# Linear attention and two expert layers on one core: a packed attention state, fewer groups of attention matmuls, other banks and other tiles for sums

## The chip, the cores and the metric

The kernel runs on one core of a Trainium2 chip. The metric is the device time of one execution in microseconds (us). TensorE (PE) has a clock with two levels, 1.2 and 2.4 GHz; the profile gives the granted share of the higher one.

## What is computed

A linear attention with a decaying state feeds a two-layer network with ELU, and that feeds four experts with ReLU, weighted by normalised probabilities. All is float32.

```python
# attention: batch 4, heads 8, 768 steps, head size 48
for t in range(S):
    state = alpha[:, :, t, :, None] * state + np.einsum('bhd,bhe->bhde', k[:, :, t], v[:, :, t])
    y[:, :, t] = np.einsum('bhd,bhde->bhe', q[:, :, t], state)
# first layer: 3072 tokens, 384 -> 2048 -> 384
h = x @ w_in
g = np.where(h > 0.0, h, np.exp(np.minimum(h, 0.0)) - 1.0)
x = g @ w_out
# second layer: 4 experts, 384 -> 1024 -> 384
p = domain_probs / (domain_probs.sum(-1, keepdims=True) + 1e-09)
for e in range(E):
    out += p[:, e:e + 1] * (np.maximum(x @ w1[e], 0.0) @ w2[e])
```

## The kernel before

**Units.** The 768 steps are cut into 6 chunks of 128. A unit is one chunk of one batch, 24 in all; each has 8 heads, two to a group of 128 partitions (head j of a pair on partitions 64j to 64j+47, the rest padding). For a unit, `prep0` to `prep2` make the running products of alpha by a scan (L181) and scale k and q with them (L198 to L208); `scores` multiplies k by q on TensorE (L218) into two banks, and VectorE masks them into `sm` (L224); `ktrans` transposes k (L235), and ScalarE copies it to `kn`; `yout_t` adds the state's part (L265) and the values' part (L272) in one bank, ScalarE copies it to `yt` (L277), it is stored to memory and read back in another layout as `xr` (L281); `state` multiplies `kn` by the values (L295) and updates the state of the batch on VectorE (L306, L308); the unit's `raw` tile is then free for the load of a later unit (L171); `xtrans` makes two halves of `xr`, a cast on ScalarE (L330) and a subtraction on VectorE (L331).

**The state** of a batch was a tile of 128 partitions x 4 pairs x 112 columns, with the two heads of a pair as diagonal blocks of 48 and zeros between, so that one matmul served both.

**First layer.** A block is one chunk of all batches, 512 tokens; it has 16 items. An item is nine matmuls of the first product (`first`, L370) into one bank of a ring of three (h0, h1, h2), the ELU (L381 to L383, and a split into `g` by ScalarE, L330, and VectorE, L331), and nine of the second product (`second`, L393) into t0 to t2, two items later. At a block's end ScalarE copies t0 to t2 to `x1raw` (L850). The units of the next chunk run between the items of a block: each has six steps, one in each half item. Weights of the first layer stand in the tiles W0 to W7 (two items each), the block's input in X0 or X1 by turns.

**Before and behind.** The four units of the first chunk run ahead of block 0, with five banks. The last block has no attention; during it GpSimd makes the 15 sums (`xs`, L497) of the first pair of chunks that the second layer multiplies, and each is split by a cast on ScalarE and a subtraction on GpSimd (`xc`). The second layer (L650, L700) uses 15 sums for 18 products; its weights are loaded by SP (`wa`, `wb`).

**Order.** TensorE's order is the program's in the first chunk and in the second layer; elsewhere a scheduler orders each engine's instructions from the program's order, its pools and its own estimates. Engines then work in order.

## Time and profile before

| | |
|---|---|
| median of 3 runs | 1308.62 us (1307.59 to 1314.47) |
| profiled execution | 1309.81 us, span 1308.1 us |
| TensorE busy | 1258.4 us, 96% |
| VectorE busy | 890.6 us, 68% |
| ScalarE busy | 582.7 us, 45% |
| GpSimd busy | 518.4 us, 40% |
| mean granted clock | 0.986 |

Times in rows are counted from the span's start. PE is the matmuls, PEld the weight loads, DVE is VectorE, ACT ScalarE, POOL GpSimd, SP the queue of loads. A matmul that follows another starts before that one has ended, so the cost of a group is read from starts: from its first start to the first start of what follows. A float32 matmul is recorded as two passes. The idle time before an instruction stands in brackets with what ended it.

### The profile page before, as it was taken

How to read it: one execution, taken by the hardware profiler on the slowest of the kernel's cores; microseconds unless marked ns; L12 is line 12 of the kernel's file. 1: busy time of each engine (PE TensorE's matmuls, PEld its weight loads, DVE VectorE, ACT ScalarE, POOL GpSimd, SP SyncE). 2: the span in 40 equal slices, each digit the busy share in tenths (PEclk: the TensorE clock that was granted, in tenths of full speed). 3: DMA queues.
4: the chain of work that ended last, by engine and by line, in shares of the span. 5: the costliest groups of instructions: out<-in, count | busy, mean ns of one | idle time of the engine just before them, and what ended most of it. 6: DMA issues, size and time to landing. Idle time of an engine off the chain costs nothing.

```text
span 1308.1 us, 17463 instructions
## 1 busy us (share of the span) xinstructions
PE 1258.4 (96%) x6297; PEld 1014.6 (78%) x6297; DVE 890.6 (68%) x1546; ACT 582.7 (45%) x1076; POOL 518.4 (40%) x405
## 2 busy tenths in 40 slices
PE   8989999999999998889999999899999999999997
PEld 5676788778778787668888888788888878888886
DVE  9999988687777742366757666566667575767664
ACT  5666666566556564433434241333333233333241
POOL 0000000000000015348878474887966465447472
PEclk9999999999999999999999999999999999999999
DMA  6545366556666541425747348765645574525232
GB/s 246 195 164 178 109 221 239 189 203 214 242 223 216 188 147 73 173 93 194 258 159 278 114 161 335 256 243 183 255 167 199 185 296 166 195 97 204 102 109 75
DMA packets 71533, 246.67 MB, mean 189 GB/s; under 512 B 6680, under 2 KB 38264, under 8 KB 62096
## 3 DMA queue, kind: packets, MB, share of 16 engines
q1 hardware_dynamic: 68016, 236.84, 50.5%
q10 hardware_dynamic: 3424, 8.65, 1.9%
q8 instruction: 51, 0.84, 0.3%
q14 instruction: 42, 0.34, 0.1%
HBM read 182.11 MB, written 63.36 MB: 188 GB/s over the span
## 4 chain that ended last, share of the span: by engine, by line
PE 65%; DMA 11%; DVE 11%; ACT 5%; POOL 5%; issue 2%; SPq 1%; ACTq 0%; DVEq 0%; POOLq 0%
PE h L650 22%; PE t L700 13%; PE a L700 9%; PE t L393 7%; PE h L370 7%; DMA wraw<-in_we_dram 5%; PE h L700 4%; DMA x0d<-yt 2%; DMA raw<-in_att_dram 2%; DVE u L670 1%; DMA xr<-x0d 1%; DVE wh L331 1%; DVE P L181 1%; POOL xs L497 1%; DVE h L383 1%
## 5 line engine op out<-in xcount | busy, mean ns | idle before, releaser
L670 DVE TENSOR_TENSOR u<-h,u 128x512 f32<-128x512 f32 x258 | 177.5, 688 | 90.4 <-PE h L650 89.4
L393 PE MATMUL t<-g,w_W 128*128 128x512 f32 x864 | 226.1, 404 | 13.1 <-ACT g L330 12.5
L370 PE MATMUL h<-x,w_W 128*128 128x512 f32 x864 | 224.0, 402 | 3.7 <-ACT w_W L330 3.7
L650 PE MATMUL h<-xc_Q,wa 128*128 128x512 f32 x780 | 219.9, 391 | 3.3 <-DVE g L331 1.4
L630 POOL TENSOR_TENSOR g_W<-c,g_W 128x512 fp32r<-128x512 f32 x128 | 164.8, 1303 | 123.6 <-ACT c L629 105.5
L393 PEld LDWEIGHTS t<-g,w_W 128*128 128x128 f32 x864 | 162.5, 192 | 53.0 <-ACT g L330 14.6
L628 ACT ACTIVATE g_W<-c 128x512 fp32r<-128x512 f32 x128 | 80.0, 626 | 274.5 <-DVE c L670 159.9
L370 PEld LDWEIGHTS h<-x,w_W 128*128 128x128 f32 x864 | 162.8, 192 | 42.5 <-ACT w_W L330 5.1
L331 POOL TENSOR_TENSOR xc_X<-xr,xc_X 128x512 fp32r<-128x512 f32 x2 | 2.6, 1300 | 478.9 <-DMA xr<-x1d 478.7
L650 PEld LDWEIGHTS h<-xc_Q,wa 128*128 128x128 f32 x780 | 145.4, 188 | 37.4 <-DVE u L670 3.8
L700 PE MATMUL t<-g_W,wb 128*128 128x512 f32 x576 | 157.6, 389 | 0.0
L700 PEld LDWEIGHTS t<-g_W,wb 128*128 128x128 f32 x576 | 108.0, 188 | 22.6 <-POOL g_W L630 0.2
L629 ACT ACTIVATE c<-c 128x512 f32<-128x512 f32 x192 | 121.0, 632 | 7.4
L670 DVE TENSOR_TENSOR c<-u,h 128x512 f32<-128x512 f32 x123 | 84.1, 686 | 50.4 <-PE h L650 38.4
L664 DVE COPY u<-h 128x512 f32<-128x512 f32 x99 | 68.1, 690 | 68.3 <-PE h L650 68.0
L700 PE MATMUL a<-g_W,wb 128*128 128x512 f32 x384 | 112.0, 391 | 0.0
L630 POOL TENSOR_TENSOR g_X<-c,g_X 128x512 fp32r<-128x512 f32 x64 | 82.5, 1303 | 62.6 <-ACT c L629 52.0
L628 ACT ACTIVATE g_X<-c 128x512 fp32r<-128x512 f32 x64 | 40.0, 626 | 142.0 <-DVE c L670 78.5
L383 DVE SCALAR_TENSOR_TENSOR h<-e,h 128x512 f32<-128x512 f32 x96 | 66.5, 692 | 49.7 <-ACT e L382 49.2
L331 DVE TENSOR_TENSOR g<-h,g 128x512 fp32r<-128x512 f32 x96 | 66.0, 687 | 37.7 <-ACT g L330 36.7
L650 PE MATMUL h<-xc_W,wa 128*128 128x512 f32 x297 | 85.0, 395 | 4.9 <-DVE u L670 2.9
L700 PEld LDWEIGHTS a<-g_W,wb 128*128 128x128 f32 x384 | 72.4, 188 | 15.4 <-POOL g_W L630 0.3
(150 smaller groups left out, 1965.1 us busy)
## 6 DMA issues: line engine op xcount, KB each, us to landing
wa<-wad SPq DMA_DIRECT2D x33, 1536.0 KB, 6.6
wb<-wbd SPq DMA_DIRECT2D x30, 1536.0 KB, 6.5
raw<-in_att_dram SPq DMA_DIRECT2D x22, 960.0 KB, 5.1
wad<-wh SPq DMA_DIRECT2D x44, 384.0 KB, 2.8
wbd<-wh SPq DMA_DIRECT2D x43, 384.0 KB, 3.4
xcd<-xh SPq DMA_DIRECT2D x30, 512.0 KB, 3.7
wraw<-in_wm_dram SPq DMA_DIRECT2D x16, 768.0 KB, 4.3
wraw<-in_we_dram SPq DMA_DIRECT2D x20, 576.0 KB, 5.3
```

The lines of the kernel that those rows point to most:

```text
L181: nc.vector.tensor_tensor_scan(P[:, a, :], raw[:, A0 + a * C:A0 + (a + 1) * C], self.plo.to_broadcast([128, C]), 1.0, ALU.mult, ALU.max,)
L331: (eng or nc.vector).tensor_tensor(out=lo, in0=src, in1=hi.bitcast(F32), op=ALU.subtract)
L370: nc.tensor.matmul(h[:, 0:n], w[:, wl, fi, k * 128:(k + 1) * 128], x[:, xl, k, n0:n0 + n], start=(k == 0 and i == 0), stop=(k == KD - 1 an ...
L383: nc.vector.scalar_tensor_tensor(out=h, in0=e, scalar=-1.0, in1=h, op0=ALU.add, op1=ALU.max)
L393: nc.tensor.matmul(self.xa[k][:, 0:n], w[:, wl, fi, DM + k * 128:DM + (k + 1) * 128], g[:, gl, 0:n], start=(f == 0 and i == 0), stop=(f == ...
L628: nc.scalar.activation(out=g[:, n, 0], in_=v, func=AF.Relu)
L629: nc.scalar.activation(out=v, in_=v, func=AF.Relu)
L630: nc.gpsimd.tensor_tensor(out=g[:, n, 1], in0=v, in1=g[:, n, 0].bitcast(F32), op=ALU.subtract)
L650: nc.tensor.matmul(b, w[:, wl], x[:, xl], start=(j == 0), stop=(j == 2))
L664: nc.vector.tensor_copy(out, b)
L670: (nc.vector if "b" in (a0, a1) or dst == "S5" else nc.gpsimd).tensor_tensor(out=out, in0=val(a0, b), in1=val(a1, b), op=ALU.add if op == ...
L700: nc.tensor.matmul(oa[m, d], wt[:, f, wl, d * 128:(d + 1) * 128], G[m][:, f, gl], start=first, stop=last)
```

## The change

The state holds 64 columns a pair, the two heads above each other on their partitions, with no zeros. The state's part of the output becomes two matmuls a pair (48 rows to 64 columns each, on separate halves of the array, into separate partitions of one bank). The state's own matmuls write 64 columns, padding included, so that its update is one addition and one product on all 128 partitions. The transposes take a bank of the first layer's ring and stand right behind the scores; `state` stands right behind `yout_t`; `prep1` one step earlier. The sums of the first pair use tile X0 in place of W1, begin in the program at the start of the last block and are spread over more of it, and W1 and X0 change places among the tiles of `xc` and `wa`. The ring of the first layer's banks shrinks to two one step later.

```diff
-            s = self.ap.tile([128, NP, SW], F32, tag=f"st{b}", name=f"st{b}")
+            s = self.ap.tile([128, NP, 64], F32, tag=f"st{b}", name=f"st{b}")
...
     def ktrans(self, u):
-        ps = self.abank()
+        ps = self.hbank()
...
         for a in range(NP):
-            nc.tensor.matmul(
-                ps[0:SW, a * C:(a + 1) * C], self.st[b][:, a, :], raw[:, Q0 + a * C:Q0 + (a + 1) * C],
-                start=(a == 0), stop=False, skip_group_check=True,
-            )
+            for j in range(2):
+                r = slice(64 * j, 64 * j + D)
+                nc.tensor.matmul(
+                    ps[64 * j:64 * j + 64, a * C:(a + 1) * C], self.st[b][r, a, :], raw[r, Q0 + a * C:Q0 + (a + 1) * C],
+                    start=(a == 0), stop=False, skip_group_check=True,
+                )
...
-        st = self.st[b]
+        st = self.st[b][:, :, 0:D]
...
-                ps[64 * j:64 * j + D, h // 2, 0:D],
-                kn[:, (h // 2) * C + 64 * j:(h // 2) * C + 64 * j + D],
+                ps[64 * j:64 * j + 64, h // 2, 0:D],
+                kn[:, (h // 2) * C + 64 * j:(h // 2) * C + 64 * j + 64],
...
+        src = ps[:, :, 0:D]
         if c:
             tmp = self.ap.tile([128, NP, D], F32, tag="tmp", name="tmp")
-        for j in range(2):
-            r, e = slice(64 * j, 64 * j + D), slice(64 * j, 64 * j + D)
-            src = ps[r, :, 0:D]
-            if c:
-                nc.vector.tensor_tensor(out=tmp[r], in0=src, in1=st[r, :, e], op=ALU.add)
-                src = tmp[r]
-            nc.vector.tensor_tensor(
-                out=st[r, :, e], in0=src, in1=pc[r].to_broadcast([D, NP, D]), op=ALU.mult
-            )
+            nc.vector.tensor_tensor(out=tmp, in0=src, in1=st, op=ALU.add)
+            src = tmp
+        nc.vector.tensor_tensor(out=st, in0=src, in1=pc.to_broadcast([128, NP, D]), op=ALU.mult)
...
-        s = [[(self.scores, (u,))]]
+        s = [[(self.scores, (u,))] + ([] if last else [(self.ktrans, (u,))])]
         s.append(N(self.prep0))
-        s.append([] if last else [(self.ktrans, (u,))])
-        s.append([(self.yout_t, (u,))] + N(self.prep1))
-        s.append([] if last else [(self.state, (u,))])
-        s[-1] += N(self.prep2)
+        s.append(N(self.prep1))
+        s.append([(self.yout_t, (u,))] + ([] if last else [(self.state, (u,))]))
+        s.append(N(self.prep2))
...
-        tmp = self.big.tile([128, 6, 512], F32, tag="W1", name="xs")
+        tmp = self.big.tile([128, 6, 512], F32, tag="X0", name="xs")
...
-        return ("Q0", "Q1", "Q2", "X0", "W0", "W5")[self.xn % 6]
+        return ("Q0", "Q1", "Q2", "W0", "W1", "W5")[self.xn % 6]
...
-        t = self.big.tile([128, 12, 2, 128], F32R, tag=("W2", "W1")[i % 2], name="wa")
+        t = self.big.tile([128, 12, 2, 128], F32R, tag=("W2", "X0")[i % 2], name="wa")
...
         def begin_x0():
-            for n, s in enumerate(self.prep_x0()):
-                at(b5 + 6 + n * 9 // 20, do, s)
-
-        at(b5 + 5, begin_x0)
+            x0 = self.prep_x0()
+            at(b5, do, x0[0])
+            for n, s in enumerate(x0[1:]):
+                at(b5 + 2 + n * 12 // 19, do, s)
+
+        at(b5 - 1, begin_x0)
...
-        self.hb = ("h0", "h1")
...
+            if i:
+                self.hb = ("h0", "h1")
```

In the changed kernel L366 and L389 are the two products of the first layer, L267, L274 and L297 the state's part, the values' part and the state, L377 and L378 the first two steps of the ELU, L327 and L328 the two halves of a split, L493 the sums.

TensorE in a unit of the third block, before, from the product behind the scores on (`a` are the attention's banks, `h` and `t` the first layer's):

```order
L370 MATMUL h_2638<-x_0_1516,w_W_874 128x512 x9
L235 MATMUL a_2655<-ident,raw 128x128 x4
L393 MATMUL t_2343<-g,w_W_748 128x512 x3
L393 MATMUL t_2344<-g,w_W_748 128x512 x3
L393 MATMUL t_2345<-g,w_W_748 128x512 x3
L265 MATMUL a_2671<-raw,st_152 112x128 x4
L272 MATMUL a_2671<-sm,raw 48x128 x8
L370 MATMUL h_2700<-x_0_1516,w_W_874 128x512 x9
L295 MATMUL a_2717<-raw,kn 48x48 x8
```

And now, from the last matmul of the scores on:

```order
L218 MATMUL a_2616<-raw 128x128
L235 MATMUL h_2629<-ident,raw 128x128 x4
L389 MATMUL t_2357<-g,w_W_652 128x512 x3
L389 MATMUL t_2358<-g,w_W_652 128x512 x3
L389 MATMUL t_2359<-g,w_W_652 128x512 x3
L366 MATMUL h_2661<-x_0_1522,w_W_874 128x512 x9
L389 MATMUL t_2357<-g,w_W_753 128x512 x3
L389 MATMUL t_2358<-g,w_W_753 128x512 x3
L389 MATMUL t_2359<-g,w_W_753 128x512 x3
L267 MATMUL a_2691<-raw,st_152 64x128 x8
L274 MATMUL a_2691<-sm,raw 48x128 x8
L297 MATMUL a_2714<-raw,kn 64x48 x8
```

The transposes moved up to the scores and into an `h` bank, and the state moved up to the output.

GpSimd at the start of the last block, now; ahead of these rows stand one sum (`xs<-xr`) and one split of an input (`xc_Q_4972<-xr`), so that the second of the pair at the end is the fifteenth of this chain:

```order
L493 TENSOR_TENSOR xs<-xr 128x512
L328 TENSOR_TENSOR xc_Q_5063<-xs,xc_Q_5063 128x512
L493 TENSOR_TENSOR xs<-xs,xr 128x512
L493 TENSOR_TENSOR xs<-xr 128x512
L328 TENSOR_TENSOR xc_Q_4898<-xs,xc_Q_4898 128x512
L493 TENSOR_TENSOR xs<-xs 128x512
L493 TENSOR_TENSOR xs<-xr,xs 128x512
L328 TENSOR_TENSOR xc_Q_4972<-xs,xc_Q_4972 128x512
L328 TENSOR_TENSOR xc_Q_4898<-xs,xc_Q_4898 128x512
L328 TENSOR_TENSOR xc_Q_4972<-xr,xc_Q_4972 128x512
L328 TENSOR_TENSOR xc_Q_4898<-xs,xc_Q_4898 128x512
L493 TENSOR_TENSOR xs<-xr 128x512 x2
```

Before, these sums stood behind the four splits that need no sum, and the chain had other tiles.

ScalarE at the end of a block's copies, before (`e<-h_4686` and `e<-h_4724` begin the ELU of two items of the last block):

```order
L381 ACTIVATE e<-h_4686 128x512
L382 ACTIVATE e<-e 128x512
L850 COPY x1raw<-t_4033 128x512
L850 COPY x1raw<-t_4034 128x512
L330 CAST g<-h_4686 128x512
L850 COPY x1raw<-t_4035 128x512
L851 DMA x1d_70<-x1raw 128x1536
L381 ACTIVATE e<-h_4724 128x512
```

And now (`e<-h_4688` and `e<-h_4749` belong to the first two items of the last block; the cast of `xc_Q_5063` just ahead of `e<-h_4749` reads the second of the pair of sums that ends the rows of GpSimd):

```order
L327 CAST xc_Q_4972<-xs 128x512
L377 ACTIVATE e<-h_4688 128x512
L327 CAST xc_Q_4898<-xs 128x512
L378 ACTIVATE e<-e 128x512
L327 CAST xc_Q_4898<-xs 128x512
L327 CAST xc_Q_5063<-xs 128x512
L327 CAST g<-h_4688 128x512
L327 CAST xc_Q_5063<-xs 128x512
L377 ACTIVATE e<-h_4749 128x512
L850 COPY x1raw<-t_4065 128x512
L378 ACTIVATE e<-e 128x512
L850 COPY x1raw<-t_4066 128x512
```

Casts of sums now stand ahead of the copies that free t0 to t2.

## Rows read from the trace of the kernel before

**Rows 1.** Busy by stage: stretch, length, PE, PEld, DVE, ACT, POOL, clock, DMA:

```profile
0.00:41.00 41.00, 34.90 (x281) 24.30 (x283) 36.35 (x76) 22.28 (x43) 1.09 (x8) 0.92 0.67 239
41.00:110.00 69.00, 61.81 (x365) 47.89 (x362) 63.87 (x105) 44.02 (x76) 0.00 (x0) 0.93 0.53 179
481.00:557.00 76.00, 67.59 (x282) 54.54 (x281) 22.14 (x32) 36.76 (x63) 33.13 (x27) 0.96 0.32 115
```

**Rows 2.** Waits of PE, 175 to 475: sum, times, longest (us):

```profile
PE a L235 <- DVE sm L224: 8.3, 5, 2.8
```

**Rows 3.** Timeline of PE, one unit: start, length, instructions:

```profile
178.38 1.16 PE L218 MATMUL a<-raw 48*128 48x128 f32 x16
179.47 2.34 PE L393 MATMUL t<-g,w_W 128*128 128x512 f32 x9
...
186.22 1.03 PE L265 MATMUL a<-raw,st 128*112 128x128 f32 x8
...
188.19 2.34 PE L370 MATMUL h<-x,w_W 128*128 128x512 f32 x9
190.46 0.56 PE L295 MATMUL a<-raw,kn 128*48 128x48 f32 x16
190.96 2.34 PE L393 MATMUL t<-g,w_W 128*128 128x512 f32 x9
```

**Rows 4.** Timeline of PE, two other units:

```profile
28.59 1.16 PE L218 MATMUL t<-raw 48*128 48x128 f32 x16 [0.51 <-PE a L248]
29.68 0.66 PE L235 MATMUL t<-ident,raw 128*128 128x128 f32 x4
...
119.67 1.08 PE L272 MATMUL a<-sm,raw 128*48 128x128 f32 x16
120.58 0.53 PE L295 MATMUL a<-raw,kn 128*48 128x48 f32 x16
121.04 1.19 PE L393 MATMUL t<-g,w_W 128*128 128x512 f32 x4
```

**Rows 5.** VectorE by line: op, count, busy us, mean ns:

```profile
L308 DVE TENSOR_TENSOR st<-tmp,P 48x192 f32<-48x192 f32 x32 | 11.3, 352 | 0.9
```

**Rows 6.** Timeline of ACT, DVE and PE, 287 to 292:

```profile
287.45 0.51 ACT L330 CAST x<-xr 128x384 fp32r<-128x384 f32 x1 [3.82 <-DMA xr<-x0d]
...
288.81 0.67 DVE L331 TENSOR_TENSOR g<-h,g 128x512 fp32r<-128x512 f32 x1
...
290.73 0.66 PE L235 MATMUL a<-ident,raw 128*128 128x128 f32 x4 [1.86 <-DVE sm L224]
```

**Rows 7.** Timeline of the SP queue, 277 to 286:

```profile
278.15 0.42 SPq L171 DMA_DIRECT2D raw<-in_att_dram  x1
284.94 0.37 SPq L281 DMA_DIRECT2D xr<-x0d  x1
```

**Rows 8.** Timeline of PE in the last block, and its waits, 474 to 575:

```profile
489.27 2.20 PE L370 MATMUL h<-x,w_W 128*128 128x512 f32 x9
...
513.75 2.20 PE L370 MATMUL h<-x,w_W 128*128 128x512 f32 x9
...
534.49 2.20 PE L370 MATMUL h<-x,w_W 128*128 128x512 f32 x9
...
PE t L393 <- ACT g L330: 8.2, 2, 4.6
```

**Rows 9.** Timeline of POOL in the last block:

```profile
505.83 2.55 POOL L497 TENSOR_TENSOR xs<-xr 128x512 f32<-128x512 f32 x2 [19.56 <-PE t L393]
508.34 1.29 POOL L497 TENSOR_TENSOR xs<-xs,xr 128x512 f32<-128x512 f32 x1
```

**Rows 10.** Timeline of ACT in the last block:

```profile
481.58 0.62 ACT L330 CAST xc_Q<-xr 128x512 fp32r<-128x512 f32 x1 [0.68 <-DMA xr<-x1d]
```

**Rows 11.** Load issues of the page: count, KB, us to landing:

```profile
wa<-wad SPq DMA_DIRECT2D x33, 1536.0 KB, 6.6
```

**Rows 12.** Timeline of PE at the start of layer 2:

```profile
560.52 1.65 PE L650 MATMUL h<-xc_Q,wa 128*128 128x512 f32 x6 [1.39 <-DVE g L331]
```

More of the change, by code (lines that the diff above doesn't have):

```diff
@@ L502, in prep_x0 @@
         x, s = {}, {}
-        tiles = [self.xc_tile() for _ in range(5)]
-        at = {p: (tiles[i // 3], i % 3) for i, p in enumerate(ORDER)}
+        tiles = []
         def loads(k):
@@ L528, in one @@
         def one(p):
-            t, i = at[p]
+            i = ORDER.index(p)
+            if i % 3 == 0:
+                tiles.append(self.xc_tile())
+            t, i = tiles[i // 3], i % 3
             y = s[p] if p in s else v[p] if p in v else x[XSUM[p][0]]
```

## The prediction

> **What bounds the kernel now.** I read the busy time by stage first [rows 1]: TensorE works 61.8 of 69 us in the stretch 41 to 110 us and 67.6 of 76 us in 481 to 557 us, so time comes from taking its waits away; but VectorE works 36.4 of the first 41 us and 63.9 of the 69 us after it, so there VectorE sets the pace. The rest of the span, from 557 us on, is the second layer, whose instructions stand in the same order on every engine after the change but for the first group and a few tile names; I leave it alone. Next the waits of TensorE between 175 and 475 us [rows 2]: one line stands out, the key transposes that wait for VectorE's masking (`sm`), 8.3 us in 5 waits. The timeline of one unit [rows 3, 4] gives the price of each group of attention matmuls. The last two places are the block 481 to 557, with 8.2 us of waits for ScalarE [rows 8], and the first step of layer 2, which waits 1.39 us for a bank [rows 12].
>
> **The span and the median.** The profiled execution took 1309.81 us with a span of 1308.1; the median of the runs is 1308.62. I sum against the profiled one and take the difference off the median.
>
> **The array's own time.** Nine matmuls of the first layer take 2.04 us (a first and a second product follow each other every 4.08 us: 489.27 to 513.75 is six such pairs, [rows 8]). Moving the transposes behind the scores costs and saves nothing: the scores take 1.09 us up to the next matmul of the layer (178.38 to 179.47, [rows 3]), and also 1.09 us up to transposes that follow them directly (28.59 to 29.68, [rows 4]), so the change of mode is only paid elsewhere. Output and state took 1.97 (186.22 to 188.19) and 0.50 us (190.46 to 190.96), together 2.47. Now the state part of the output is made of eight matmuls on two 48-row halves instead of four on the whole array, in the form of the scores; if pairs run side by side as there, it takes 1.09 us. The values part takes 0.91 (119.67 to 120.58) and the state right behind it 0.46 (120.58 to 121.04), as the one unit shows in which they already stood together [rows 4]. That is 2.46: nothing gained inside. What goes is one exit and one entry: 188.19 to 190.46 is 2.27 for nine matmuls, 0.23 over. The split state part brings an entry of its own, about half of that. So 16 units gain 0.1 to 0.15 each, the four last ones (no state) lose about 0.2 each, and in the first block, where the scheduler puts pieces of first-layer products between the pieces of two units, I count a loss of up to 1. I take -1, bounds -3 and +1.
>
> The pairing is the unknown: no row shows two row halves that write different partitions of one bank. The scores pair two row halves into two banks; the values part pairs two column halves in one bank. Both run paired, so I take paired. Unpaired, the eight pairs (1.09 less the change of mode, 0.2, is 0.89) take 0.89 more, over 20 units 17.8 us.
>
> The rows show pairs of row halves only with a bank each. The Trainium skill (TensorEngine Tiling (Array Packing), Restrictions and Gotchas, "Gotcha 1: PSUM Pressure") says more: row tiles must write to different banks and cannot be in one bank at the same time. No run shows it either way; by that rule the unpaired price holds, which is the first rival.
>
> **VectorE.** A state update on two halves was two products of 0.352 us [rows 5] and two additions of the same shape, which I count alike; on all 128 partitions it is one of each. In the first chunk a unit loses one product (4 x 0.352 = 1.4 us before 41 us); each of the 16 later units loses 0.704. VectorE is the bound up to 110 us and somewhat beyond, where four of these lie: 2.8. Later the saving is covered by VectorE's own slack. 4.2 us is the most; as the order there changes on all engines, I take -3, bounds -5 and +3.
>
> **The transposes' bank.** Before, they took one of two banks that the scores had just filled, and so waited for the mask. Now they take a bank of the first layer, which is free: the 8.3 us go. What is late next is the same bank pool. With the transposes in the ring of three, the second product group after the scores finds its bank used by the group just ahead of the scores, and must wait until VectorE's subtraction of that group has read it. In the unit at 290 us that subtraction starts at 288.81 and takes 0.67, ending at 289.48 [rows 6]; TensorE would be there 1.86 us before 290.73 plus the 0.4 of the transposes that it has done earlier, at 289.3: 0.2 us of wait in place of 1.86. The subtraction is late since ScalarE, and VectorE with it, stood behind the cast of `xr`, 3.82 us [rows 6]. That cast waits for a store and a read through memory: the raw load goes out at 278.15, the read of `xr` only at 284.94 [rows 7], since the store queues with the load's 128 x 1920 floats. Merging output and state lets the raw load go out 2 to 3 us sooner, as soon as the state has read its tile; the store then finds the load further on. On the other side the new ScalarE order puts that cast ahead of the exponential, which delays the group by 1 us if `xr` is no earlier, and where the store used to go ahead of the load it now goes behind. So 0 to 1.3 us a unit stay in some six units. I take 1.3 in all and -7; bounds -8.3 (nothing stays) and -2 (each pays most).
>
> SP's queue matters here: `xr` now stands behind one store of converted weights, which waits for VectorE; that store is ready sooner than the attention store lands, so I give it nothing.
>
> **The sums of the first pair.** Before, GpSimd could not start them until 505.83 [rows 9], when weights tile W1 was free, and ScalarE stood in order behind them: TensorE lost 34.49 less two periods, 534.49 - 513.75 - 8.16 = 12.6 us, of which 8.2 are waits [rows 8] and the rest the granted clock, 0.96 of the stage [rows 1]. Now they use X0, free after the block's predecessor, so GpSimd can start when the first inputs are in: ScalarE's first cast that waits for `xr` starts at 481.58 [rows 10]. GpSimd needs 1.255 us an instruction (505.83 to 508.34 is two, [rows 9]). The order decides the rest. ScalarE's cast of `xc_Q_5063<-xs` that stands just ahead of `e<-h_4749` needs the fifteenth instruction of GpSimd: 481.6 + 15 x 1.255 = 500.4. Behind it on ScalarE come that activation and then the copy `x1raw` of bank t0, each 0.6: t0 is free at about 502.2, t2 at 503.8. The second product of the block's first group starts in t0, and TensorE reaches it at 491.31 (489.27 plus 2.04). So it waits 10.9 us, in one piece, and ends at 504.5 instead of 493.35: 11.1 lost. The clock, which read 0.96 over this stage with two waits of four us, will have fallen: 1 to 2.5 us more. That makes 12.1 to 13.6 against 12.6: I take 0, bounds -1.5 and +3. No other wait follows: the casts into W0 and W1 stand where their sums have long been made. On SP the weight load into X0 now stands ahead of the other `wa` and waits for GpSimd's last read of the sums, its thirtieth instruction, at about 520 us; it, the other and two `wb` behind it take under 7 us each [rows 11] and are needed from 557 on, so they are covered, by some 9 us.
>
> **The first step of layer 2** keeps three banks instead of two, so the 1.39 us wait [rows 12] goes. The step after it reuses the bank of the step before once, about 1 us for VectorE. I take -1; bounds -1.4 and 0.
>
> **Sum:** -1 - 3 - 7 + 0 - 1 = -12. 1309.81 becomes 1297.8, the median 1308.6 becomes **1296.6**; I say 1296.5. Adding the bounds in the same direction is too wide; half of their widths gives 1288 to 1304 for this case alone.
>
> **Rivals.** (1) Slower: the two row halves do not run together in one bank. 17.8 us on top of the sum: 1314. It decides from some two thirds of the 17.8 on, when the gain of 12 is eaten. For it: no row shows this form. Against it: the halves' outputs lie on different partitions, as in the values part, which pairs. (2) The bank wait only moves: the groups behind the transposes wait as long as the transposes did, and VectorE's saving is lost in the new order; -1 and -1 remain: 1306.5. For it: both engines stand in order behind the cast of `xr`, and the new order puts that cast earlier. Against it: VectorE works less and the raw load is earlier. (3) The sums do what they were moved for: ScalarE's order does not bind and the 12.6 us go as well: 1284. For it: GpSimd starts 24 us sooner. Against it: the fifteenth instruction and the copy behind it, above.
>
> **How the numbers follow.** The forecast 0.66, rival (1) 0.08, rival (2) 0.19, rival (3) 0.07. Faster by over 0.5% (below 1302.1, about what a measurement of this kernel can tell from no change): most of the forecast, 0.62, and rival (3), 0.07: 0.69. Slower by over 0.5% (above 1315.2): part of rival (1), 0.04. The rest, 0.27, lies between. The range 1284 to 1307 leaves out rival (1), a third of rival (2) and half of rival (3), under 2 in 10.
>
> **What would show it.** Right: no wait of the transposes for `sm`; waits of the second group after the scores for VectorE's subtraction, together under 3 us; a raw load within 0.5 us of the output's end and the `xr` read near seven us after it; a unit's state part in pairs some 0.11 us apart, one after the other; VectorE with half the state updates at the same 0.35 us; one wait of about 11 us at the first second product of the last block, behind `x1raw`, with the clock at half speed after it; layer 2 as long as before. Wrong: single starts 0.11 us apart in the state part (rival 1), long waits of first products for banks (rival 2), a last block without a wait (rival 3), or a first 120 us that is longer than before, which would say that VectorE's work was not the bound there.

## The result, and the profile after

The changed kernel took 1297.93 us (median of 4 runs, 1294.08 to 1298.62); the kernel before beside it 1309.99. The ratio is 0.9898, with a 95% interval of 0.9863 to 0.9933. A second series gave 0.9928 (0.9904 to 0.9952, 12 runs). The forecast was 1296.5, with a range of 1284 to 1307. The sum came out; its terms did not all come out, so the hit is in part luck, and that is what the rest is about.

Cut at the starts of three groups of matmuls (first product of the first layer, of its second block, of its last block) and at the first group of layer 2, the span reads as follows. Both kernels were profiled twice.

| stretch | before | changed | difference of the means |
|---|---|---|---|
| first chunk | 39.99, 40.07 | 42.56, 43.05 | +2.8 |
| block 0 | 99.71, 98.80 | 92.98, 92.63 | -6.5 |
| blocks 1 to 4 | 341.41, 340.40 | 336.35, 336.25 | -4.6 |
| last block, to layer 2 | 79.41, 80.16 | 78.95, 77.55 | -1.5 |
| layer 2 and end | 747.58, 747.67 | 745.78, 747.05 | -1.2 |

Busy time by these stretches in the kernel before, first execution (columns as in [rows 1]: length, PE, PEld, DVE, ACT, POOL, granted clock, DMA share, GB/s):

```profile
0.00:39.99 39.99, 33.89 (x271) 23.53 (x271) 35.52 (x75) 21.60 (x43) 1.09 (x8) 0.91 0.66 235
39.99:139.70 99.71, 90.13 (x527) 69.17 (x527) 92.47 (x153) 61.45 (x105) 0.00 (x0) 0.93 0.48 163
139.70:481.11 341.41, 332.37 (x2018) 267.25 (x2017) 260.19 (x570) 210.00 (x446) 0.66 (x1) 1.00 0.60 208
```

The same in the changed kernel, first execution:

```profile
0.00:42.56 42.56, 38.05 (x271) 26.56 (x271) 33.45 (x71) 21.68 (x43) 1.09 (x8) 0.84 0.60 212
42.56:135.54 92.98, 86.42 (x559) 66.39 (x559) 88.72 (x145) 60.65 (x106) 0.00 (x0) 1.00 0.52 179
135.54:471.89 336.35, 329.87 (x2145) 266.35 (x2144) 251.77 (x545) 207.53 (x445) 0.00 (x0) 1.00 0.61 211
471.89:550.84 78.95, 68.19 (x289) 55.91 (x288) 22.20 (x33) 38.16 (x66) 33.61 (x27) 0.91 0.32 116
```

Length less PE's busy time is what TensorE waited. In blocks 1 to 4 that went from 9.0 to 6.5 us, in block 0 from 9.6 to 6.6. In block 0 the clock matters as much: at 0.93 of 99.71 us up to 7.0 us were lost to it, at 1.00 none. The first chunk goes the other way, 0.91 to 0.84: up to 6.8 us lost in place of 3.6. From the start to block 1 the clock cost up to 10.6 and 6.6 us in the two executions of the kernel before, and 6.8 and 6.9 in the changed one.

The gain of 4.6 us in blocks 1 to 4 is less firm than the table looks. Three kernels of the experiments below have the order of instructions of one of the two in blocks 0 to 4. First the kernel before with the sums alone changed, then the changed kernel with the splits on VectorE, and with sums and splits there, each in blocks 1 to 4:

```profile
134.40:473.92 339.52, 332.03 (x2018) 267.40 (x2016) 261.77 (x573) 209.57 (x446) 0.00 (x0) 0.99 0.60 210
```

```profile
135.20:474.27 339.07, 331.32 (x2146) 267.58 (x2144) 251.96 (x545) 207.53 (x445) 0.00 (x0) 0.99 0.61 210
134.16:475.63 341.47, 332.83 (x2145) 268.66 (x2144) 252.32 (x545) 207.79 (x445) 0.00 (x0) 0.99 0.61 208
```

The old order thus waited 9.0, 6.8 and 7.5 us, the new one 6.5, 6.0, 7.8 and 8.6, and over these seven executions the stretch differs by 2.2 us and not by 4.6. In block 0 the same seven give 95.96 to 99.71 us against 92.63 to 93.10.

The waits of TensorE in blocks 1 to 4, changed kernel (sum, times, longest), which answer [rows 2]:

```profile
PE h L366 <- DVE g L328: 5.6, 4, 2.0
PE t L389 <- DVE g L328: 0.8, 2, 0.5
```

The 8.3 us of the transposes are gone, and 6.4 us stand in their place, at the next product groups. One unit, on PE, answers [rows 3]:

```profile
277.56 1.16 PE L218 MATMUL a<-raw 48*128 48x128 f32 x16
...
278.65 0.66 PE L235 MATMUL h<-ident,raw 128*128 128x128 f32 x4
...
287.69 1.09 PE L267 MATMUL a<-raw,st 48*64 48x128 f32 x16
...
288.71 1.08 PE L274 MATMUL a<-sm,raw 128*48 128x128 f32 x16
...
289.62 0.62 PE L297 MATMUL a<-raw,kn 128*64 128x48 f32 x16
...
290.17 2.14 PE L389 MATMUL t<-g,w_W 128*128 128x512 f32 x8
```

Scores to transposes 1.09, state part 1.02 (287.69 to 288.71), values part 0.91, state 0.55. The state part's eight pairs run side by side.

### The profile page after: what moved, and what is told of

Read it like the earlier page. It is cut to its first block, busy times and chain, and to the rows that moved or that the text cites. A ratio compares the mean times of both kernels' runs of the same rounds, so it can differ in the third digit from the quotient of the medians.

```text
span 1296.6 us, 17731 instructions
## 1 busy us (share of the span) xinstructions
PE 1252.3 (97%) x6457; PEld 1013.4 (78%) x6457; DVE 876.4 (68%) x1510; ACT 579.5 (45%) x1076; POOL 518.5 (40%) x405
## 4 chain that ended last, share of the span: by engine, by line
PE 68%; DMA 10%; DVE 10%; POOL 4%; ACT 4%; issue 3%; SPq 1%; ACTq 0%; DVEq 0%; POOLq 0%
PE h L648 22%; PE t L698 13%; PE a L698 9%; PE h L366 7%; PE t L389 7%; PE h L698 4%; DMA x0d<-yt 3%; DMA raw<-in_att_dram 2%; DMA wraw<-in_we_dram 2%; DMA xr<-x0d 1%; DVE wh L328 1%; DVE u L668 1%; DVE h L379 1%; DVE g L328 1%; PE a L267 1%
## 5 line engine op out<-in xcount | busy, mean ns | idle before, releaser
L389 PE MATMUL t<-g,w_W 128*128 128x512 f32 x864 | 220.3, 396 | 16.0 <-ACT x1raw L850 10.8
L366 PE MATMUL h<-x,w_W 128*128 128x512 f32 x864 | 218.5, 395 | 7.8 <-DVE g L328 5.6
L389 PEld LDWEIGHTS t<-g,w_W 128*128 128x128 f32 x864 | 161.4, 189 | 53.9 <-ACT x1raw L850 11.2
L493 POOL TENSOR_TENSOR xs<-xr 128x512 f32<-128x512 f32 x8 | 10.1, 1274 | 471.0 <-DMA xr<-x1d 471.0
L366 PEld LDWEIGHTS h<-x,w_W 128*128 128x128 f32 x864 | 160.3, 189 | 45.6 <-DVE g L328 7.3
L648 PE MATMUL h<-xc_W,wa 128*128 128x512 f32 x390 | 110.2, 391 | 4.6 <-DVE u L668 2.6
L628 POOL TENSOR_TENSOR g_X<-c,g_X 128x512 fp32r<-128x512 f32 x64 | 82.7, 1304 | 62.6 <-ACT c L627 51.7
L648 PEld LDWEIGHTS h<-xc_W,wa 128*128 128x128 f32 x390 | 72.7, 188 | 22.2 <-DVE u L668 4.0
L328 DVE TENSOR_TENSOR g<-h,g 128x512 fp32r<-128x512 f32 x96 | 65.9, 687 | 30.5 <-ACT g L327 30.2
```

Of the source, the lines that this page charges most:

```text
L328: (eng or nc.vector).tensor_tensor(out=lo, in0=src, in1=hi.bitcast(F32), op=ALU.subtract)
L366: nc.tensor.matmul(h[:, 0:n], w[:, wl, fi, k * 128:(k + 1) * 128], x[:, xl, k, n0:n0 + n], start=(k == 0 and i == 0), stop=(k == KD - 1 an ...
L389: nc.tensor.matmul(self.xa[k][:, 0:n], w[:, wl, fi, DM + k * 128:DM + (k + 1) * 128], g[:, gl, 0:n], start=(f == 0 and i == 0), stop=(f == ...
L628: nc.gpsimd.tensor_tensor(out=g[:, n, 1], in0=v, in1=g[:, n, 0].bitcast(F32), op=ALU.subtract)
L648: nc.tensor.matmul(b, w[:, wl], x[:, xl], start=(j == 0), stop=(j == 2))
```

## The experiments

Each kernel differs from one of the two by the edit shown. Medians and ratios are against runs of the kernel before on the same chip in the same series; 91 such runs have a median of 1309.2 us and a mean granted clock of 0.9864, and the changed kernel's 16 runs 1298.8 us and 0.9893.

| kernel | runs | median | ratio (95%) |
|---|---|---|---|
| before, bank of the transposes alone | 10 | 1306.34 | 0.9993 (0.997 to 1.0015) |
| before, packed state alone | 7 | 1318.14 | 1.0079 (1.0049 to 1.0108) |
| before, sums alone | 10 | 1309.09 | 0.9998 (0.9976 to 1.002) |
| changed, old steps of a unit | 10 | 1305.89 | 0.996 (0.9937 to 0.9983) |
| changed, state update in halves | 10 | 1311.44 | 1.0009 (0.9983 to 1.0035) |
| changed, two tiles for the running products | 10 | 1303.80 | 0.996 (0.9936 to 0.9984) |
| the same, raw loads held back | 4 | 1289.39 | 0.9854 (0.9822 to 0.9885) |
| changed, splits on VectorE | 6 | 1295.25 | 0.9897 (0.9864 to 0.993) |
| changed, sums and splits on VectorE | 4 | 1288.05 | 0.9815 (0.9771 to 0.9859) |
| both groups of edits | 4 | 1285.20 | 0.981 (0.9771 to 0.985) |

### The bank of the transposes alone

```diff
     def ktrans(self, u):
-        ps = self.abank()
+        ps = self.hbank()
```

> The kernel before with one edit: the key transposes take a bank of the first layer's ring, at their old step. Theory (the bank frees the transposes and part of the wait moves to the ring): no wait of the transposes for the masking is left in 175 to 475 us (8.3 us before), and waits of first products for VectorE's subtraction of 3 to 7 us appear in their place; the time falls by 1 to 5 us, to 1304 to 1308. Rival (the wait simply goes): no such new waits, about 8 us less, near 1300. Rival (it moves whole): as much wait as before, 1308 to 1310.

Its waits of TensorE in blocks 1 to 4:

```profile
PE h L370 <- DVE g L331: 5.2, 4, 2.5
PE t L393 <- DVE g L331: 0.9, 1, 0.9
PE t L393 <- ACT g L330: 0.3, 1, 0.3
```

6.4 us of new waits for 8.3 of old ones, as the first theory had it; the time is not told from the kernel before. Over three executions of the old code the waits for `sm` were 8.3, 6.8 and 7.5 us, so by the waits the bank by itself is worth 0.4 to 1.9 us, 1.1 on the mean.

### The packed state alone, and the changed kernel with the old steps

```diff
-            s = self.ap.tile([128, NP, SW], F32, tag=f"st{b}", name=f"st{b}")
+            s = self.ap.tile([128, NP, 64], F32, tag=f"st{b}", name=f"st{b}")
...
-        for j in range(2):
...
+        nc.vector.tensor_tensor(out=st, in0=src, in1=pc.to_broadcast([128, NP, D]), op=ALU.mult)
```

> The kernel before with the packed state alone: two matmuls a pair for the state's part of the output, 64 columns a pair, one addition and one product for the update; old steps, old banks, old sums. Theory (VectorE sets the pace up to 110 us): VectorE's busy time falls by 36 x 0.35 = 12.6 us, and the stretch from the first product of the first layer to the start of its second block, 99.7 us before, shortens by 2 to 4 us beyond what the granted clock explains; the rest stays: 1304 to 1307. Rival (the stretch is set by the granted clock, which fell five times in it before and not once after): no shortening where the clock is as low as before, 1307 to 1310. State part in pairs, with no extra 0.9 us a unit.

Blocks 1 to 4 of this kernel (busy time), the wait of its transposes, and the longest of them on VectorE and TensorE:

```profile
130.81:482.05 351.24, 337.42 (x2146) 266.76 (x2144) 252.23 (x549) 209.78 (x446) 0.66 (x1) 0.99 0.59 203
```

```profile
PE a L235 <- DVE sm L224: 13.0, 8, 4.0
```

```profile
266.78 1.37 DVE L181 TENSOR_TENSOR_SCAN P<-raw,plo 128x128 f32<-128x128 f32 x4 [5.11 <-DMA raw<-in_att_dram]
...
270.01 1.12 PE L235 MATMUL a<-ident,raw 128*128 128x128 f32 x4 [3.96 <-DVE sm L224]
```

A miss for both theories: slower than before by 0.8%. Two things are in the rows. TensorE's busy time is 5.0 us over the 332.37 of before, of which the clock can be 3.5 (0.01 of 351): so 1.5 to 5.0 us are the price of the split state part on its own. And the transposes wait for the mask longer, 13.0 us, although VectorE works less (252.2 against 260.2 us): in the engines' new order the mask stands behind other work that waits for a transfer, at 266.78 behind a scan that waits 5.11 us for its raw tile. In block 0 this kernel takes 93.79 us at a clock of 0.98, so a part of the gain there is with it.

```diff
-        s = [[(self.scores, (u,))] + ([] if last else [(self.ktrans, (u,))])]
+        s = [[(self.scores, (u,))]]
         s.append(N(self.prep0))
-        s.append(N(self.prep1))
-        s.append([(self.yout_t, (u,))] + ([] if last else [(self.state, (u,))]))
-        s.append(N(self.prep2))
+        s.append([] if last else [(self.ktrans, (u,))])
+        s.append([(self.yout_t, (u,))] + N(self.prep1))
+        s.append([] if last else [(self.state, (u,))])
+        s[-1] += N(self.prep2)
```

> The changed kernel with the old six steps of a unit: the transposes (in the first layer's bank) and the state each on its own between groups of first-layer matmuls. Theory (each group of attention matmuls costs TensorE a way in and out, so the merging pays and the split state part by itself costs): TensorE's own time in the four blocks after the first, waits taken off, is 4 to 7 us longer, near the 73.7 us over the first layer's matmuls that the packed state alone has, against 67.5 of the changed kernel; the bank waits stay at 5 to 8 us; time 1302 to 1306. Rival (the merging is worth little, and the gain is VectorE's and the bank's): under 2 us longer, 1297 to 1300.

Its blocks 1 to 4:

```profile
133.71:480.10 346.39, 337.49 (x2145) 267.78 (x2144) 252.16 (x546) 210.43 (x446) 0.04 (x1) 0.99 0.59 206
```

7.6 us more of TensorE's busy time than the 329.87 of the changed kernel; the clock (0.01 of 346) can be 3.5 of that, so 4 to 7.6 us are the matmuls' own. The waits are 8.9 us against 6.5. The two groups a unit thus carry the packed state: without them it costs TensorE more than it brings.

### VectorE's work given back

```diff
-        nc.vector.tensor_tensor(out=st, in0=src, in1=pc.to_broadcast([128, NP, D]), op=ALU.mult)
+        for j in range(2):
+            r = slice(64 * j, 64 * j + 64)
...
+            nc.vector.tensor_tensor(out=st[r], in0=src, in1=pc[r].to_broadcast([64, NP, D]), op=ALU.mult)
```

> The changed kernel with the state's update in two halves again (64 partitions each, two additions and two products), so that VectorE alone has its old work back: 36 more instructions of 0.35 us, 12.6 us. Theory of the prediction (VectorE sets the pace up to 110 us): the time from the start to the second block of the first layer, 135.5 us, grows by 2 to 4 us at the same granted clock. Rival (nothing there rests on VectorE's sum of work; the gain in this stretch was the clock): it stays within 1 us at the same clock; time 1296 to 1299.

Busy time in block 0 and in blocks 1 to 4, and then the timeline at a wait in block 2, on VectorE, ScalarE and TensorE:

```profile
41.36:137.11 95.75, 88.92 (x560) 67.15 (x559) 90.76 (x149) 61.16 (x105) 0.00 (x0) 0.98 0.50 174
137.11:482.55 345.44, 332.88 (x2146) 268.69 (x2144) 262.25 (x573) 208.57 (x445) 0.00 (x0) 0.99 0.60 206
```

```profile
246.77 1.37 DVE L181 TENSOR_TENSOR_SCAN P<-raw,plo 128x128 f32<-128x128 f32 x4 [5.87 <-DMA raw<-in_att_dram]
...
248.17 0.63 ACT L187 ACTIVATE lnP<-P 128x512 f32<-128x512 f32 x1 [6.16 <-DVE P L181]
...
249.24 1.22 PE L370 MATMUL h<-x,w_W 128*128 128x512 f32 x2 [4.30 <-DVE g L332]
```

The start of block 1 moves by 1.6 us (137.11 against 135.54) at nearly the same clock (0.88 and 0.98 in the two stretches up to there, against 0.84 and 1.00), under the 2 to 4 of the theory and over the rival's 1. The surprise is later: in blocks 1 to 4 TensorE waits 12.6 us instead of 6.0 to 8.6, and the whole advantage over the kernel before is gone. Not all of it is VectorE's arithmetic. The edit moves VectorE's order too, and the row at 246.77 shows the form of the loss: a scan stands in order ahead of the subtraction that TensorE needs, waits 5.87 us for its raw tile to land, and ScalarE stands behind the scan. How the loss divides between work and order was not separated. In block 0 the waits are 6.8 us (95.75 less 88.92), hardly more than the 6.2 to 6.6 of the changed order.

### Where the remaining bank wait comes from

In the changed kernel the waits look like this, on SP, ACT, DVE and PE:

```profile
271.68 0.48 SPq L171 DMA_DIRECT2D raw<-in_att_dram  x1
272.53 0.79 ACTq L281 DMA_DIRECT2D x0d<-yt  x2
...
278.84 1.37 DVE L181 TENSOR_TENSOR_SCAN P<-raw,plo 128x128 f32<-128x128 f32 x4 [1.78 <-DMA raw<-in_att_dram]
...
279.15 0.37 SPq L283 DMA_DIRECT2D xr<-x0d  x1
...
281.74 0.52 ACT L327 CAST x<-xr 128x384 fp32r<-128x384 f32 x1 [0.86 <-DMA xr<-x0d]
282.16 0.63 ACT L378 ACTIVATE e<-e 128x512 f32<-128x512 f32 x1
...
284.66 0.69 DVE L328 TENSOR_TENSOR g<-h,g 128x512 fp32r<-128x512 f32 x1
...
285.40 2.36 PE L366 MATMUL h<-x,w_W 128*128 128x512 f32 x9 [1.98 <-DVE g L328]
```

Two suspects stand ahead of `g`: the cast of `xr`, with the second step of the ELU right behind it (282.16), and a scan that had waited 1.78 us for a raw load. Both stand so ahead of three of the four long waits (200, 285 and 372 us); ahead of the fourth (329) VectorE and ScalarE stood waiting for a load of weights. The first edit takes the scan out of the way, the second also the load:

```diff
-        P = self.ap.tile([128, NP, C], F32, tag="P", name="P", bufs=3)
+        n = u[0] * B + u[1]
+        m = n % 3 if n < B else (n + 1) % 2 if n > B else 1
+        P = self.ap.tile([128, NP, C], F32, tag=f"P{m}", name="P")
```

> The changed kernel with one edit: the running products of alpha of the later units have two tiles by turns instead of three, so that a unit's scan can't stand ahead of the previous unit's state. Seen in the trace of the changed kernel: each of the long bank waits left (1.76 us at 198, 2.14 at 283, 1.32 at 328, 1.14 at 371 us) follows a scan that waited 0.2 to 1.8 us for its raw tile to land, with ScalarE's logarithm behind it and the first layer's exponential behind that. Theory A (this scan, hoisted to the landing of its load, makes ScalarE late): the waits of 7.4 us in 175 to 475 us fall under 2 us and the four blocks after the first shorten by 4 to 6 us; time 1291 to 1294. Theory B (the cast of xr, which waits for a store and a read, makes it late by itself, as the prediction had it): the waits stay at 5 to 8 us, 1296 to 1299.

```diff
+            if c * B + b > B + 2:
+                self.nc.gpsimd.tensor_copy(t[0:1, 0:1], self.xl[0:1, 0, 0:1])
             self.nc.sync.dma_start(out=t, in_=self.att[c, b])
...
-        y = self.y.pop(u)
+        y = self.xl = self.y.pop(u)
```

> The kernel of the run with two tiles for the running products, and with the raw loads of the later units held back: GpSimd copies one element of xr into the raw tile first, so that the load starts only when the read of xr has landed. Theory (the store before xr queues with the raw load, and ScalarE's cast of xr, which waits for both transfers, makes the first layer's ELU late): from the issue of the store to the issue of the xr read it takes 2 to 3.5 us instead of 4 to 6.3, the bank waits in the four blocks after the first fall from 7.5 to 1 to 4 us, and these blocks take 332 to 336 us. Rival (other transfers, of the weights of layer 2 above all, hold the store just as long, or the scan now waits for the later landing): the waits stay at 6 us or more.

The wait in blocks 1 to 4, first with the scan gated alone, then with the loads held back as well, and of the latter a piece of the timeline (the queues of ScalarE and SP, and GpSimd):

```profile
PE h L368 <- DVE g L330: 6.9, 5, 2.5
```

```profile
PE h L370 <- DVE g L332: 4.0, 3, 2.7
```

```profile
270.27 1.50 ACTq L285 DMA_DIRECT2D x0d<-yt  x2
...
274.52 0.37 SPq L287 DMA_DIRECT2D xr<-x0d  x1
...
277.24 0.17 POOL L172 COPY raw<-xr 1x1 f32<-1x1 f32 x1 [18.98 <-DMA xr<-x0d]
277.44 0.33 SPq L173 DMA_DIRECT2D raw<-in_att_dram  x1
```

The scan is not the cause: with it gated the wait is as long, since ScalarE then stands longer in front of the cast (its waits for `xr` between 135 and 472 us go from 6.9 to 19.2 us in all). The transfers are: with the load behind the read of `xr`, the store at 270.27 is through by 274.52 (4.3 us, against 6.6 from 272.53 to 279.15 above). From the second half's store to the read, the twelve units of blocks 1 to 3 average 3.7 us, against 4.6 with the scan gated alone and 5.0 in the changed kernel; the waits fall to 4.0 us (4.4 in the kernel with both groups of edits), blocks 1 to 4 to 334.52, and the time to 1289.39, of which 5.4 us come from the last block (73.58 us, with 6.5 us of wait for `x1raw` in that order). The second edit moves the order of VectorE and ScalarE too, and that share was not taken apart. As far as that goes, the prediction's chain (store, load, read, cast) holds. What it got wrong is that the change would shorten it: before, the average was 4.6. The first edit by itself measured slower than the changed kernel (1303.80); its blocks 1 to 4 took 339.17 us and its last block 83.31, where the wait for `x1raw` was 12.8 us. Why that wait differs between these two was not followed up.

### The sums of the first pair

The sums' part of the change alone, on the kernel before (tile X0, the early start, the tiles changed round):

```diff
-        tmp = self.big.tile([128, 6, 512], F32, tag="W1", name="xs")
+        tmp = self.big.tile([128, 6, 512], F32, tag="X0", name="xs")
...
-        at(b5 + 5, begin_x0)
+            x0 = self.prep_x0()
+            at(b5, do, x0[0])
+            for n, s in enumerate(x0[1:]):
+                at(b5 + 2 + n * 12 // 19, do, s)
+
+        at(b5 - 1, begin_x0)
```

> The kernel before with the sums of the first pair alone changed (tile X0, earlier in the program, spread; the tiles of the inputs and of a weight changed round). Theory (ScalarE stands in order behind GpSimd's 1.255 us instructions): the two waits of 3.7 and 4.6 us in the last block become one wait of 10 to 12 us of the first second product behind the copies x1raw, followed by half the clock; the block loses 12 to 14.5 us against 12.6, so the time is 1308 to 1311. Rival (the sums are spread enough): no wait, 1296 to 1298.

One wait of 10.2 us behind `x1raw`, where two stood [rows 8], and the same time. In the changed kernel, first the PE rows at the start of the last block, then POOL's and ACT's:

```profile
480.05 2.20 PE L366 MATMUL h<-x,w_W 128*128 128x512 f32 x9
493.02 4.21 PE L389 MATMUL t<-g,w_W 128*128 128x512 f32 x9 [10.76 <-ACT x1raw L850]
...
550.84 1.52 PE L648 MATMUL h<-xc_Q,wa 128*128 128x512 f32 x6
```

```profile
472.74 1.29 POOL L493 TENSOR_TENSOR xs<-xr 128x512 f32<-128x512 f32 x1 [471.00 <-DMA xr<-x1d]
...
488.87 2.47 POOL L493 TENSOR_TENSOR xs<-xr 128x512 f32<-128x512 f32 x2
```

```profile
491.37 0.62 ACT L327 CAST xc_Q<-xs 128x512 fp32r<-128x512 f32 x1 [6.23 <-POOL xs L493]
491.90 0.59 ACT L377 ACTIVATE e<-h 128x512 f32<-128x512 f32 x1
492.39 0.58 ACT L850 COPY x1raw<-t 128x512 f32<-128x512 f32 x1
```

The chain is there link by link: GpSimd's fifteenth instruction ends at 491.3, the cast starts at 491.37, the copy at 492.39, the second product at 493.02, at half clock (4.21 instead of 2.20 us for nine matmuls). Two edits take the chain apart:

```diff
-            self.split(t[:, i, 0], t[:, i, 1], y, nc.gpsimd)
+            self.split(t[:, i, 0], t[:, i, 1], y)
```

> The changed kernel with one edit: in the last block the 15 subtractions that split the sums go to VectorE instead of GpSimd, which keeps the 12 additions and subtractions of the sums. Theory (the 10.8 us wait is the length of GpSimd's chain ahead of ScalarE's cast, fifteen instructions of 1.255 us): about eight or nine instructions stand ahead now, so the wait shrinks to 2 to 5 us, the clock stays high or falls less, and the time is 1286 to 1291. Rival (the wait comes from something else, such as the loads of the sums' inputs or the copies themselves): the wait stays near 10 us, 1296 to 1299.

The wait is 6.8 us, longer than the 2 to 5 expected, because GpSimd's instructions became longer (last section): nine stand ahead of the cast and take 14.4 us, 1.6 each; by an estimate at the 1.255 of before the wait would have been 3.7. With the sums on VectorE as well:

```diff
-            self.sum_x(nc.gpsimd, s[p], p, x, s)
+            self.sum_x(nc.vector, s[p], p, x, s)
...
-                self.sum_x(nc.gpsimd, v[p], p, x, s)
+                self.sum_x(nc.vector, v[p], p, x, s)
```

> The changed kernel with all 12 sums and all 15 splits of the last block on VectorE, none on GpSimd. With the splits alone moved, the wait fell from 10.8 to 6.8 us. Theory (the wait is the length of the chain of sums ahead of ScalarE's casts): a sum takes 0.69 instead of 1.26 us and fewer casts stand ahead of the copies x1raw, so the wait is 0 to 3 us, the clock doesn't fall in this block, and the block takes 67 to 71 us against 79; time 1286 to 1291. Rival (VectorE's own work is then late, since the sums stand in order among the steps of the ELU): the first wait is gone, but waits of second products for VectorE of 3 us or more take its place; 1293 to 1297.

```profile
475.63:540.91 65.28, 65.28 (x289) 54.07 (x288) 37.79 (x60) 37.65 (x66) 0.00 (x0) 1.00 0.39 139
```

The last block has no wait left: TensorE busy 65.28 of 65.28 us, VectorE 37.79. The block is 13.7 us shorter than in the changed kernel.

### Both together

> All sums and splits of the last block on VectorE, two tiles for the running products and the raw loads held back behind the read of xr, on the changed kernel. Theory: the gains add, the 11 to 14 us of the last block and 3 to 6 us of the bank waits: 1281 to 1286. Rival (the held loads give nothing, or the clock falls elsewhere): 1287 to 1291.

1285.20 us, 0.981 of the kernel before. Blocks 0 to 4 take 426.03 us (429.33 in the changed kernel) and the last block 66.89 (78.95), 15.4 less together; by the medians it is 13.6. It beats both kernels.

### Both kernels once more

> The kernel before once more, unchanged, for a second profiled execution. Theory (its long waits make the granted clock fall in the first block of the first layer): the stretch from the first product to the second block again has 3 to 14 us at half clock, takes 95 to 100 us, and its waits are again 8 to 10 us with one of 2 us or more. Rival (the clock in the first profile was chance): no half clock there, about 93 us. From the start of the second block to the last one 338 to 342 us.

> The changed kernel once more, unchanged, for a second profiled execution and more timed ones. Theory (shorter waits keep the clock up in the first block): no more than 3.5 us at half clock in that block, 92.5 to 94.5 us, mean granted clock of all runs at least 0.002 above that of the kernel before; the ratio stays at 0.988 to 0.993. Rival (chance): as much half clock there as in the kernel before, and the same mean clock.

Block 0 and blocks 1 to 4, second execution of the kernel before, then of the changed one:

```profile
40.07:138.87 98.80, 88.13 (x528) 66.71 (x528) 92.62 (x154) 61.26 (x105) 0.00 (x0) 0.97 0.48 169
138.87:479.27 340.40, 333.63 (x2018) 268.93 (x2016) 260.15 (x570) 210.33 (x447) 0.65 (x1) 0.99 0.60 209
```

```profile
43.05:135.68 92.63, 86.39 (x559) 66.41 (x559) 88.59 (x145) 60.54 (x106) 0.00 (x0) 1.00 0.51 180
135.68:471.93 336.25, 330.21 (x2145) 267.47 (x2144) 252.13 (x545) 207.56 (x445) 0.00 (x0) 0.99 0.61 212
```

The clock of block 0 is hardly chance: 0.93, 0.97 and 0.96 (sums alone) in the old order, 1.00 four times in the changed one, whose longest wait there is 1.4 us against 2.3 and 2.4. That the shorter waits are the reason is not shown: the kernel with the scan gated has 0.98 there with no wait over 1.4 us. The mean clock of all runs is 0.0029 higher. Among the 91 runs of the kernel before, 0.001 of mean clock goes with 0.75 us, so by an estimate this is worth about 2.2 us.

## Why the prediction was right, point by point

**The array.** Forecast -1. In blocks 1 to 4 the changed kernel's matmuls take 329.87 us at a clock of 1.00; the old ones, in the kernel with the bank alone and also at 1.00, 331.52: -1.65. In block 0 busy time fell by 2.7 on the mean while the clock gave up to 5.0 (the mean of 0.07 x 99.71 and 0.03 x 98.80), so the pieces cost up to 2.3 more there; I had put 1. About right in sum, but its parts were both too small and cancel: a way in and out at 0.23 us is 2.8 us for the twelve units with a state in blocks 1 to 4, where the merging is worth 4 to 7.6 and the split state part alone costs 1.5 to 5.0. The state part in pairs came out as forecast, 1.02 us against 1.09, so rival (1) falls. The Trainium skill's rule that row tiles can't be in one bank at the same time (TensorEngine Tiling (Array Packing), Restrictions and Gotchas, "Gotcha 1: PSUM Pressure") does not hold for this form: the eight pairs write two halves of the partitions of one bank in 1.02 us, where one after the other would have been near 1.9.

**VectorE.** Forecast -3 up to 110 us and nothing later. In block 0 the waits fell by 3.7 us on the mean (9.6 and 10.7 to 6.6 and 6.2; a third execution of the old order had 8.1). That VectorE's arithmetic is the reason is not shown: the packed state alone brings them to 5.9, but with the old arithmetic given back to the changed kernel they are 6.8 and not 10, and block 1 starts 1.6 us later. The premise that VectorE's sum of work sets the pace up to 110 us is thus borne out for about half of the term, 1.6 of 3 us. In the first chunk 1.4 was forecast, and the gain is about 0.5: at a clock of 1.00 it took 37.47 us with the old update and 37.02 and 36.82 with the new one, in three of the experiments; the changed kernel's 42.6 and 43.0 are the clock's, 0.84. That the saving is covered later was wrong as far as it was tested: with the old work given back, blocks 1 to 4 wait 4 to 6.6 us more, though order and work were not separated there.

**The transposes' bank.** Forecast -7, measured -1.6 (waits in blocks 1 to 4: 9.0 and 6.8 before, 6.5 and 6.0 after), and only -0.5 over all seven executions of the two orders. This is the term that was mis-sized, and the step that failed is "the store then finds the load further on". The load goes out sooner, but in the unit shown less than 1 us ahead of the store (271.68 and 272.53), so the two still share the transfers: 5.0 us from store to read, against 4.6. The 0 to 1.3 us a unit that I left "in some six units", 1.3 in all, are 5.6 us in four waits of up to 2.0. The bounds, -8.3 and -2, just miss it. So rival (2) was near the truth on this term, and in three of the four long waits for the reason that it gave, the cast of `xr`; its 1306.5 was too high since the rest of the gain stayed.

**The sums.** Forecast 0, with one wait of 10.9 us behind `x1raw`. Measured: one wait of 10.8 (10.3 in the second execution), then half clock. Without the start of layer 2 the block takes 76.2 us on the mean in both kernels. The fifteenth instruction was the right one to count, and moving the arithmetic off GpSimd showed it. Rival (3) falls.

**The start of layer 2.** Forecast -1. From the last second product to the first group went from 3.59 us (556.93 to 560.52) to 2.04 (548.80 to 550.84): the wait of [rows 12] is gone. The next 17.80 us took 18.82 before, so it is -2.6 in all, over the bound of -1.4: a third bank helped the groups behind the first as well, in spite of a new wait of 2.1 us for VectorE.

**What was not in the sum.** The profiles differ by 11.0. The waits are 3.7 and 1.6 of it, layer 2 is 2.6, the last block 0. The 3.1 left are the array and the clock together; 2.2 is the clock by the estimate from all runs, so about 0.9 for the array. The forecast hit by luck: a bank term 5.4 us too large stood in for 2.2 us of clock, 1.6 more at layer 2 and 0.7 more of waits in block 0.

**Two slips of the working.** In the sums' part 34.49 is the end of the time 534.49; the difference meant, 534.49 - 513.75 - 8.16 = 12.6, is right. And half of the bounds' widths is 1293 to 1305 about 1296.5, not 1288 to 1304; the measured time lies in both.

## What to carry to other kernels

A bank that is free takes a wait away from one group and hands it to the next group that uses the ring; what is gained is only the distance to the instruction that really comes late. Follow that instruction back to its transfer: here the load of a later unit delays a store that ScalarE stands waiting for, and holding the load back gained more in these blocks than the bank. Where an engine's order is fixed, count the slow engine's instructions ahead of the one that is waited for; that count gave 10.9 us for 10.8, and moving the arithmetic to the engine with time to spare took the whole of it away.

## What the runs showed of the hardware

VectorE and GpSimd slow each other down. With the splits on VectorE beside GpSimd's sums, seven splits on VectorE took 1412 ns on the mean, and with GpSimd idle 692; the sums took up to 1.7 us instead of 1.27. VectorE's line of the splits (count, busy us, mean ns), first beside GpSimd, then with GpSimd idle:

```profile
L328 DVE TENSOR_TENSOR xc_Q<-xs,xc_Q 128x512 fp32r<-128x512 f32 x7 | 9.8, 1412 | 2.0 <-ACT xc_Q L327 1.8
```

```profile
L328 DVE TENSOR_TENSOR xc_Q<-xs,xc_Q 128x512 fp32r<-128x512 f32 x7 | 4.8, 692 | 0.0
```

The Trainium skill (GPSIMD Engine Reference, 1. Specifications) says that GpSimd shares its interfaces to SBUF with VectorE, with contention where VectorE has two inputs in SBUF, which the split has; the trace agrees, with twice the time. A split on VectorE whose `h` stands in a bank took 0.68 us beside the same sums (at 478.19, while GpSimd was at a sum from 477.80 to 479.43).

The first chunk, which has the same number of matmuls in every kernel here, took 36.8 to 43.1 us, in step with its granted clock: 36.82, 37.02 and 37.47 at 1.00, 38.4 to 40.1 at 0.91, 41.0 to 41.4 at 0.88, 42.5 to 43.1 at 0.84. A change of 2 us in such a stretch can't be read from one execution of each kernel. Why the changed kernel has the lower clock there more often stays open.
